# Keys' and queries' parts in an order that lets two of three come from DRAM in one transfer

## The chip, the cores and the metric

The kernel runs on one core of a Trainium2 chip. A core has a matrix engine (TensorE, PE in the profile, with its weight loads as PEld), a vector engine (DVE), a scalar engine (ACT), a general engine (POOL) and SyncE (SP), which here issues transfers. They run side by side, each in the order of its own queue, and wait for each other by semaphores. Transfers are moved by 16 DMA engines that all queues share. The metric is the time of one execution on the device in microseconds; less is better.

## What is computed

Two layers, each an attention block and a dense block with Mish, on 2048 tokens of width 512, with 32 heads of 16 columns each, in float32:

```python
def _A_ref(x, wqkv, wo):
    B, S, D = x.shape
    H = 32
    Dh = D // H
    qkv = (lambda x, *d: x.transpose(*d))((x @ wqkv).reshape(B, S, 3, H, Dh), 2, 0, 3, 1, 4)
    q, k, v = qkv[0], qkv[1], qkv[2]
    scores = jnp.einsum("bhqd,bhkd->bhqk", q, k) * (Dh ** -0.5)
    p = _softmax(scores, axis=-1)
    o = jnp.einsum("bhqk,bhkd->bhqd", p, v)
    return (lambda x, *d: x.transpose(*d))(o, 0, 2, 1, 3).reshape(B, S, D) @ wo
...
x = A_x
x = x + _A_ref(_layernorm(x, axis=-1), A_wqkv, A_wo)
x = x + _B_ref(_layernorm(x, axis=-1), B_w1, B_b1, B_w2)
x = x + _A_ref(_layernorm(x, axis=-1), A_wqkv, A_wo)
x = x + _B_ref(_layernorm(x, axis=-1), B_w1, B_b1, B_w2)
```

## The kernel before

**Numbers in two parts.** To keep float32's accuracy with the matrix engine's faster type, a number is split into a high part and a low part (the rest). A product is then the sum of three: high by high, high by low and low by high. For keys and queries the three are put below each other in the contraction: a head has 16 columns, so its keys take 48 rows and its queries 48 rows (`KROWS`), and one matmul sums all three products. `K_PARTS` and `Q_PARTS` (lines 37 and 38) say which part stands in which 16 rows: keys high, high, low and queries high, low, high. Two more rows (48 and 49, up to `MROWS` = 50) bring the row maximum into the score: ones on the keys' side, and the negated maximum, in two parts, on the queries' side.

**Projection (`qkv`, line 470).** Matmuls over the normed input make a 128x512 block of the transposed queries (m = 0 to 3) or keys (m = 4 to 7); each block holds 8 heads. `evict` (line 488) splits it into its two parts on the scalar and the vector engine and the scalar engine issues its store to `scr[m]`, a DRAM tensor of [2, 128, 2048]: part, row, token. Values go to `vscr` in the same manner.

**Loading a group (`prep_qk`, line 232).** Four heads make a group; there are 8 groups in a layer. Two heads share a tile: one in partitions 0 to 49, the other in 64 to 113. For each head SP issues a transfer of ones (line 244) and three transfers of 16 rows for the keys and three for the queries (line 251). The first group is loaded inside `qkv`, in two pieces: tokens 0 to 1535 as soon as three of the four token blocks of both `scr[0]` and `scr[4]` are stored, and the last 512 when the fourth is. Groups 1 to 7 are loaded during the group before, in `run` (line 420): `prep_qk` is a generator, and from the eighth of a group's 64 steps on, one transfer is issued in each step.

**The attention loop (`run`).** A step is one block of 512 queries by 128 keys for four heads; 16 steps make a block, four blocks a group, 512 steps a layer. Three streams are interleaved by hand in the order of `CYCLE`: row maxima (`max_pair` and `max_one`: a 128x512 score matmul at line 275, reduced by the vector engine at lines 293 and 308), scores with exponentials (line 355 on the matrix engine, 357 on the scalar engine), and products with the values (line 402). The maxima run 22 steps ahead (`AHEAD`). When a block's maxima are complete, `max_rows` (line 324) transposes them, SP writes them to DRAM (line 332, `rows<-nt`) and reads them back into rows 48 and 49 of the query tiles (line 337, `qs<-rows`); the block's scores need them.

**Order.** `Order` chains the instructions of TensorE, DVE and ACT in the order of the program. Transfers aren't chained: the compiler's scheduler places them in SP's queue by its own simulation, so that those of `prep_qk` may stand before or behind the transfers of rows.

**Layer 0 also prepares weights.** `make` (line 113) loads a block of weights, splits it, and the scalar engine issues its store; this is done at sixteen of the attention loop's steps in layer 0.

Of the kernel before, what the change touches and what calls it, by code (L numbers as in the profile page):

```python
# [10 lines left out]
F32 = mybir.dt.float32  # L11
# [9 lines left out]
S, D, H, DH, F = 2048, 512, 32, 16, 1792  # L21
NCH = 4
# [11 lines left out]
KROWS = 48  # L34
MROWS = 50
HALF = 64
K_PARTS = (0, 0, 1)
Q_PARTS = (0, 1, 0)
CYCLE = "QvXXvQMXvvXM"
TAIL_START = "QvvRvv"  # L40
TAIL = "WQRvvv"
# [10 lines left out]
def kernel(ctx: ExitStack, tc: tile.TileContext, x, wqkv, wo, w1, b1, w2, out):  # L52
    nc = tc.nc
# [20 lines left out]
    def b8(shape, dt, name):  # L74
        return blk.tile(shape, dt, tag="blk", name=name)
# [140 lines left out]
    class Attention:  # L216
# [15 lines left out]
        def prep_qk(self, g, first=0, last=S):  # L232
            l = self.l
            if g not in self.qk:
                self.qk[g] = [
                    [b8([P, S], F32R, f"{n}s{l}{g}{u}") for u in range(HG // 2)] for n in ("k", "q")
                ]
            for u in range(HG // 2):
                k, q = self.qk[g][0][u], self.qk[g][1][u]
                m, h0 = divmod(g * HG + 2 * u, P // DH)  # L240
                for e in range(2):
                    r0 = e * HALF
                    if first == 0:
                        nc.sync.dma_start(
                            k[r0 + KROWS : r0 + MROWS].bitcast(F32).rearrange("p (r n) -> p r n", n=256),
                            ones[:, None, :].to_broadcast([MROWS - KROWS, S // 256, 256]),
                        )
                        yield
                    for t, parts, base in ((k, K_PARTS, NCH), (q, Q_PARTS, 0)):
                        for j, a in enumerate(parts):  # L250
                            nc.sync.dma_start(
                                t[r0 + j * DH : r0 + (j + 1) * DH, first:last].bitcast(F32),
                                self.scr[base + m][a, (h0 + e) * DH : (h0 + e + 1) * DH, first:last].bitcast(F32),
                            )
                            yield

        def prep_v(self, g):
            va = b8([P, NKT, HG, VW], F32, f"va{self.l}{g}")
# [352 lines left out]
    def norm_steps(src, nm, got, key, tag, o):  # L611
        st = tmp.tile([P, NCH, 6], F32, tag="st", name=f"st{nm}")
        mv = tmp.tile([P, NCH, 2], F32, tag="mv", name=f"mv{nm}")
        ve = tmp.tile([P, NCH], F32, tag="ve", name=f"ve{nm}")
        rs = tmp.tile([P, NCH], F32, tag="rs", name=f"rs{nm}")
        for t in range(NCH):
            o(nc.vector.bn_stats(st[:, t], src[:, t]))
            o(nc.vector.bn_aggr(mv[:, t], st[:, t]))
            o(nc.vector.tensor_scalar(ve[:, t : t + 1], mv[:, t : t + 1, 1], EPS, None, op0=ALU.add))
            nc.gpsimd.tensor_tensor(rs[:, t : t + 1], ve[:, t : t + 1], mhalf[:, t : t + 1], op=ALU.pow)  # L620
            yield
        th = b8([P, KT, CW], F32R, f"th{nm}")
        tl = b8([P, KT, CW], F32R, f"tl{nm}")
        got[key] = (th, tl)
        xns, tps = {}, {}
        for t in range(NCH + 2):
            if t < NCH:
                xns[t] = t512("f", f"xn{nm}{t}")
                o(
                    nc.vector.tensor_scalar(  # L630
                        xns[t], src[:, t], mv[:, t, 0:1], rs[:, t : t + 1], op0=ALU.subtract, op1=ALU.mult
                    )
                )
            if t >= 2:
                hi, sp = tps.pop(t - 2)
                o(nc.vector.tensor_tensor(tl[:, :, ts(t - 2, P)], sp, hi.bitcast(F32), op=ALU.subtract))
            if 1 <= t <= NCH:
                xn, tp = xns.pop(t - 1), pbank(tag, f"tp{nm}{t - 1}")
                for k in range(KT):
                    o(nc.tensor.transpose(tp[:, ts(k, P)], xn[:, ts(k, P)], ident))  # L640
                sp = tp.rearrange("p (k n) -> p k n", k=KT)
                hi = th[:, :, ts(t - 1, P)]
                nc.scalar.activation(hi, sp, AF.Copy)
                tps[t - 1] = (hi, sp)
            yield
# [159 lines left out]
    for l in range(2):  # L805
# [18 lines left out]
        hooks, parts, work = {}, {}, {}  # L824
# [38 lines left out]
        first = norm_steps(x2s[0], f"m{l}0", tts, 0, "s", o)  # L863
# [32 lines left out]
        if l == 0:  # L896
            last = NCH - 1
# [37 lines left out]
```

## Time and profile before

| | |
|---|---|
| median of 3 runs | 3466.72 us (3463.46 to 3468.94) |
| the profiled execution, its time | 3467.81 us |
| its span | 3466.0 us |
| granted TensorE clock | 0.997 |
| HBM read, written | 149.43 MB, 92.27 MB |
| mean DMA rate over the span | 71 GB/s |

The span runs from the first to the last instruction. In a row of a group of instructions stand the line, the engine, the operation, the tiles as output<-inputs, the count, the duration and the idle time ahead of it. A name such as `ks<-scr` says that a transfer goes from `scr` to a tile of keys; SPq and ACTq are the sequencers that issue them. PEldq EVENT_SEMAPHORE is a wait of TensorE's queue ahead of a weight load, whose length tells how long it waited. The DMA share is the mean busy share of the 16 engines.

### The profile page before, as it was taken

How to read it: one execution, taken by the hardware profiler on the slowest of the kernel's cores; microseconds unless marked ns; L12 is line 12 of the kernel's file. 1: busy time of each engine (PE TensorE's matmuls, PEld its weight loads, DVE VectorE, ACT ScalarE, POOL GpSimd, SP SyncE). 2: the span in 40 equal slices, each digit the busy share in tenths (PEclk: the TensorE clock that was granted, in tenths of full speed). 3: DMA queues.
4: the chain of work that ended last, by engine and by line, in shares of the span. 5: the costliest groups of instructions: out<-in, count | busy, mean ns of one | idle time of the engine just before them, and what ended most of it. 6: DMA issues, size and time to landing. Idle time of an engine off the chain costs nothing.

```text
span 3466.0 us, 71144 instructions
## 1 busy us (share of the span) xinstructions
PE 3443.8 (99%) x29075; PEld 1917.8 (55%) x29075; DVE 2966.5 (86%) x4155; ACT 2620.2 (76%) x4865; POOL 282.1 (8%) x329
## 2 busy tenths in 40 slices
PE   9999999999999999999999999999999999999999
PEld 6644444444444445888876444444444444458887
DVE  5699999999999996665537999999999999966554
ACT  3189899989889888356522888988998999874665
POOL 1000000000000001222200000000000000012222
PEclk9999999999999999999999999999999999999999
DMA  7641312213121114500264202112020221154000
GB/s 253 233 102 35 81 43 74 61 54 81 45 58 50 37 55 109 195 13 13 86 199 156 53 15 46 26 36 43 18 56 15 46 37 25 55 136 167 13 13 25
DMA packets 131864, 247.39 MB, mean 71 GB/s; under 512 B 30929, under 2 KB 72401, under 8 KB 116433
## 3 DMA queue, kind: packets, MB, share of 16 engines
q1 hardware_dynamic: 77680, 169.43, 19.6%
q10 hardware_dynamic: 53856, 73.41, 5.8%
q8 instruction: 229, 3.75, 0.5%
q14 instruction: 99, 0.80, 0.1%
HBM read 149.43 MB, written 92.27 MB: 70 GB/s over the span
## 4 chain that ended last, share of the span: by engine, by line
PE 95%; DMA 2%; DVE 2%; ACT 1%; SPq 0%; issue 0%; DVEq 0%; ACTq 0%
PE pv L402 32%; PE sp L355 25%; PE pm L275 8%; PE pn L275 4%; PE h L165 3%; PE h L166 3%; PE h L164 3%; PE mo L164 3%; PE mo L165 3%; PE mo L166 3%; PE qk L164 1%; PE qk L165 1%; PE qk L166 1%; PE va L164 1%; PE va L166 1%; PE va L165 1%
## 5 line engine op out<-in xcount | busy, mean ns | idle before, releaser
L357 ACT ACTIVATE p<-sp 128x512 f32<-128x512 f32 x4040 | 2108.7, 599 | 240.9 <-PE pn L275 145.6
L308 DVE TENSOR_REDUCE mxv<-pn 128x1 f32<-128x512 f32 x2048 | 1306.2, 677 | 6.2 <-PE pn L275 4.4
L293 DVE TENSOR_REDUCE mxv<-pm 128x2 f32<-128x1024 f32 x1024 | 1241.8, 1213 | 78.6 <-PE pm L275 78.6
L355 PE MATMUL sp<-qs,ks 50*128 50x512 f32 x4040 | 1265.9, 445 | 0.0
L402 PE MATMUL pv<-p,va 128*32 128x256 f32 x16384 | 1211.7, 388 | 1.1 <-DVE pt L152 1.1
L355 PEld LDWEIGHTS sp<-qs,ks 50*128 50x128 f32 x4040 | 562.8, 184 | 689.2 <-ACT p L357 620.2
L275 PE MATMUL pn<-ks,qs 48*128 48x512 f32 x2048 | 824.8, 450 | 1.2 <-DVE mxv L308 0.9
L402 PEld LDWEIGHTS pv<-p,va 128*32 128x32 f32 x16384 | 385.0, 108 | 558.1 <-issue 428.4
L275 PE MATMUL pm<-ks,qs 48*128 48x512 f32 x2048 | 437.6, 423 | 1.4 <-DMA ks<-scr 1.4
L275 PEld LDWEIGHTS pn<-ks,qs 48*128 48x128 f32 x2048 | 366.2, 183 | 8.3 <-DVE mxv L308 2.7
L275 PEld LDWEIGHTS pm<-ks,qs 48*128 48x128 f32 x2048 | 193.5, 185 | 64.4 <-issue 7.8
L320 POOL CAST nh<-nm 128x16 fp32r<-128x16 f32 x64 | 12.6, 197 | 2436.7 <-DVE nm L315 2436.7
L666 POOL TENSOR_TENSOR hb<-hb,he 128x512 f32<-128x512 f32 x112 | 148.3, 1324 | 471.9 <-DVE he L663 471.9
L164 PE MATMUL mo<-w,ah 128*128 128x512 f32 x448 | 175.5, 392 | 3.2 <-ACT ah L669 3.0
L166 PE MATMUL h<-thm,w 128*128 128x512 f32 x448 | 175.0, 391 | 0.0
L165 PE MATMUL h<-tlm,w 128*128 128x512 f32 x448 | 174.9, 390 | 0.0
L165 PE MATMUL mo<-w,ah 128*128 128x512 f32 x448 | 174.9, 390 | 0.0
L164 PE MATMUL h<-thm,w 128*128 128x512 f32 x448 | 174.7, 391 | 0.0
L166 PE MATMUL mo<-w,al 128*128 128x512 f32 x448 | 166.1, 390 | 0.0
L668 DVE TENSOR_TENSOR hb<-hb,hr 128x512 f32<-128x512 f32 x112 | 77.3, 690 | 98.9 <-ACT hr L665 73.2
L151 ACT ACTIVATE pt<-qk 128x512 fp32r<-128x512 f32 x64 | 37.9, 598 | 147.7 <-PE qk L166 122.1
L660 ACT ACTIVATE hb<-h,b1t 128x512 f32<-128x512 f32 x112 | 76.9, 686 | 95.4 <-PE h L166 54.1
(133 smaller groups left out, 2590.2 us busy)
## 6 DMA issues: line engine op xcount, KB each, us to landing
scr<-pt ACTq DMA_DIRECT2D x64, 512.0 KB
ks<-scr SPq DMA_DIRECT2D x168, 128.0 KB
qs<-scr SPq DMA_DIRECT2D x168, 128.0 KB
vscr<-vst ACTq DMA_DIRECT2D x32, 512.0 KB
va<-vscr SPq DMA_DIRECT2D x16, 1024.0 KB
w<-w1p SPq DMA_DIRECT2D x14, 1024.0 KB
w<-w2p SPq DMA_DIRECT2D x14, 1024.0 KB
raw<-ot SPq DMA_DIRECT2D x256, 32.0 KB
```

The source lines that it names most:

```text
L164: pe(nc.tensor.matmul(acc, ah, bh, start=first and i == 0, stop=False))
L165: pe(nc.tensor.matmul(acc, ah, bl, start=False, stop=False))
L166: pe(nc.tensor.matmul(acc, al, bh, start=False, stop=last and i == n - 1))
L275: nc.tensor.matmul(out, qs[h // 2][rows, q0 : q0 + P], ks[h // 2][rows, ts(c, 512)], start=True, stop=True)
L293: self.order(nc.vector.tensor_reduce(self.mxs[b][:, 0:2, qt, c], pm, axis=AX.X, op=ALU.max))
L308: self.order(nc.vector.tensor_reduce(self.mxs[b][:, h, qt, c : c + 1], pm, axis=AX.X, op=ALU.max))
L355: nc.tensor.matmul(sp, ks[h // 2][rows, ts(kt, P)], qs[h // 2][rows, ts(qb, CW)], start=True, stop=True)
L357: return lambda: self.order(nc.scalar.activation(self.pts[s][:, h], sp, AF.Exp, scale=SCALE))
L402: nc.tensor.matmul(acc[ts(h, VW), cols], va[:, kt, h, :], self.pts[s][:, h, cols], start=kt == 0 and half == 0, stop=kt == NKT - 1, skip_g ...
L660: nc.scalar.activation(hb, acc, AF.Identity, bias=b1t[:, f : f + 1])
L666: nc.gpsimd.tensor_tensor(hb, hb, e, op=ALU.mult)
L668: nc.vector.tensor_tensor(hb, hb, r, op=ALU.mult)
```

## The change

In `prep_qk` the 16-row parts take another order: the keys' rows hold high, low, high, and the queries' rows high, high, low. The three products summed by the matmul are the same, and so are all tiles and matmuls. For each head and side, the high and the low part are now read from `scr` in one transfer, whose source is [2, 16, columns] and whose target is 32 neighbouring rows (rows 0 to 31 of the keys, rows 16 to 47 of the queries); a second transfer of 16 rows brings the high part again. So there are two transfers for each head and side where there were three.

```diff
-K_PARTS = (0, 0, 1)
-Q_PARTS = (0, 1, 0)
...
-                    for t, parts, base in ((k, K_PARTS, NCH), (q, Q_PARTS, 0)):
-                        for j, a in enumerate(parts):
-                            nc.sync.dma_start(
-                                t[r0 + j * DH : r0 + (j + 1) * DH, first:last].bitcast(F32),
-                                self.scr[base + m][a, (h0 + e) * DH : (h0 + e + 1) * DH, first:last].bitcast(F32),
-                            )
-                            yield
+                    for t, base, both, again in ((k, NCH, 0, 2 * DH), (q, 0, DH, 0)):
+                        src = self.scr[base + m][:, (h0 + e) * DH : (h0 + e + 1) * DH, first:last].bitcast(F32)
+                        nc.sync.dma_start(t[r0 + both : r0 + both + 2 * DH, first:last].bitcast(F32), src)
+                        yield
+                        nc.sync.dma_start(t[r0 + again : r0 + again + DH, first:last].bitcast(F32), src[0])
+                        yield
```

In the loop, each transfer is still issued in a step of its own, so a group's loads take 20 steps where they took 28.

## The prediction

> **What bounds the kernel now.** I read the page first, then the stages around each transfer that changes.
>
> ```profile
> PE 3443.8 (99%) x29075; PEld 1917.8 (55%) x29075; DVE 2966.5 (86%) x4155; ACT 2620.2 (76%) x4865; POOL 282.1 (8%) x329
> ...
> PE 95%; DMA 2%; DVE 2%; ACT 1%; SPq 0%; issue 0%; DVEq 0%; ACTq 0%
> ```
>
> TensorE is busy 99% of the span and is 95% of the chain that ended last; DMA is 2%. So removing transfers can gain little, and anything that holds TensorE up is lost in full, because its order is fixed by hand (`Order`). The span is 3466.0 us, the profiled run took 3467.8 us, 1 us over the median of 3466.72 us.
>
> The same is seen by stage. The columns are length, busy time of each engine, clock, DMA share and GB/s:
>
> ```profile
> 58.00:107.00 49.00, 47.25 (x209) 36.42 (x209) 14.99 (x21) 9.83 (x17) 0.00 (x0) 1.00 0.99 322
> 1763.00:1802.00 39.00, 38.55 (x178) 31.40 (x177) 11.00 (x17) 10.24 (x18) 0.00 (x0) 1.00 0.89 269
> ...
> 1412.00:1432.00 20.00, 20.00 (x90) 16.57 (x89) 15.19 (x29) 6.61 (x11) 4.99 (x4) 1.00 0.96 397
> ```
>
> ```profile
> 324.00:475.00 151.00, 151.00 (x1546) 68.27 (x1548) 150.86 (x202) 135.74 (x261) 11.81 (x14) 1.00 0.24 55
> ```
>
> Inside a group (324 to 475) PE and DVE are full and the DMA engines a quarter busy. While the first group's keys and queries are fetched, the DMA engines are full (0.99 in layer 0, 0.89 in layer 1). Hence one engine moves 322/(16 x 0.99) = 20.3 GB/s in that mix, and 397/(16 x 0.96) = 25.8 GB/s with long rows (1412 to 1432).
>
> **What the change removes.** The DMA view gives the transfers:
>
> ```profile
> ks<-scr SPq DMA_DIRECT2D x168, 128.0 KB
> qs<-scr SPq DMA_DIRECT2D x168, 128.0 KB
> ...
> qs<-scr SPq DMA_DIRECT2D x24, 96.0 KB
> ks<-scr SPq DMA_DIRECT2D x24, 96.0 KB
> ...
> qs<-scr SPq DMA_DIRECT2D x24, 32.0 KB
> ks<-scr SPq DMA_DIRECT2D x24, 32.0 KB
> ```
>
> That is 432 transfers; of each three, two become one of double size, so 144 go: 288 remain, half of them double. Bytes, matmuls, and evictions stay; the three products are the same with two of them swapped in the sum. The issue of one costs SP:
>
> ```profile
> L251 SPq DMA_DIRECT2D qs<-scr x216: 302/413/1872, 58.1 to 2859.0; - x108
> L251 SPq DMA_DIRECT2D ks<-scr x216: 302/418/1886, 62.4 to 2855.4; - x108
> ...
> who waited for it (us, times):
>   ACT pt L151: 7.6, 3
> ...
>   PE pm L275: 1.4, 1
> ```
>
> 144 x 0.415 = 60 us of SP's time, but SP sits waiting: 1207 us for the maxima's transpose alone.
>
> ```profile
> SPq L332 <- DVE nt L329: 1207.1, 64, 24.7
> ```
>
> The only wait of TensorE on these transfers is 1.4 us, once. So what is removed is worth 0 to 1.4 us.
>
> **What it adds.** Now each transfer's outermost extent is its 16 rows, on both sides. The merged one reads DRAM as [2, 16, columns]: outermost extent 2, into 32 rows. If the work is dealt out along the outermost extent, only 2 of the 16 DMA engines get any. No row here shows a long transfer of that shape, so I bound it. Over 16 engines a merged 256 KB transfer is 16,384 B an engine, 0.6 us at 25.8 GB/s. Over two it is 131,072 B, 5.1 us (6.5 at 20.3). I take two: the only shape that differs from all long transfers of the trace is the one that would have to be cut along its 16 rows instead of along its first extent, on one side alone. [...]
>
> *First group, layer 0.* SP issues, and the matmuls that need the data:
>
> ```profile
> 58.15 2.31 SPq L251 DMA_DIRECT2D qs<-scr  x5
> 62.40 2.64 SPq L251 DMA_DIRECT2D ks<-scr  x6
> ...
> 95.93 2.44 SPq L251 DMA_DIRECT2D qs<-scr  x3
> ```
>
> ```profile
> 67.80 0.47 PE L275 MATMUL pm<-ks,qs 48*128 48x512 f32 x1 [1.42 <-DMA ks<-scr]
> ```
>
> ```profile
> 84.92 0.49 PE L275 MATMUL pn<-ks,qs 48*128 48x512 f32 x2
> ```
>
> ```profile
> 106.81 0.50 PE L275 MATMUL pm<-ks,qs 48*128 48x512 f32 x2
> ```
>
> The first maximum at 67.80 already waits for its data. The one at 84.92 needs heads 2 and 3, the one at 106.81 the last 512 columns. Eight merged transfers of 192 KB put 98,304 B on each of the two engines, 4.8 us at 20.3 GB/s; eight of 64 KB put 32,768 B, 1.6 us: together 51 us, and the sixteen single ones 3 us more. From 58.15 they are through at 112, 5 us behind the need at 106.81, if nothing else ran there. The rest of that window, (322 GB/s x 49 us - 3.1 MB)/16 = 0.79 MB an engine, is 39 us more, which would make it 44 us late. I take the middle, **25 us**; part of it comes early, at 67.80, where three merged transfers stand ahead instead of a few short ones. What waits behind the stalled maximum is all of TensorE's queue, and DVE's reduction with it.
>
> *First group, layer 1.* The transfers start at 1762.85, the maxima later:
>
> ```profile
> 1762.85 3.13 SPq L251 DMA_DIRECT2D qs<-scr  x6
> ...
> 1800.06 1.55 SPq L251 DMA_DIRECT2D qs<-scr  x3
> ```
>
> ```profile
> L275 PE MATMUL pm<-ks,qs x12: 493/493/493, 1819.5 to 1837.6; 48*128 48x512 f32 x12
> ```
>
> Six pairs 3.6 us apart: the fourth, which needs the last columns, is at 1830.4. The same 54 us give 1817, in time; with the other (269 x 39 us - 3.1 MB)/16 = 0.46 MB, 23 us, 1840, 10 us late. In both layers the scalar engine issues the stores of `scr` and was held up by these loads already (7.6 us, three times, above): loads that land later hold evictions, and so TensorE, longer. Bounds 0 and 25; I take **10 us**.
>
> *Groups 1 to 7, both layers (14 times).* The burst for group 2:
>
> ```profile
> 359.20 1.70 SPq L332 DMA_DIRECT2D rows<-nt  x4
> 361.01 0.82 SPq L251 DMA_DIRECT2D qs<-scr  x2
> 362.06 1.12 SPq L337 DMA_DIRECT2D qs<-rows  x4
> 363.22 2.00 SPq L251 DMA_DIRECT2D qs<-scr  x4
> ...
> 373.94 0.68 SPq L244 DMA_DIRECT2D ks<-ones  x1
> 374.66 1.32 SPq L251 DMA_DIRECT2D ks<-scr  x3
> 376.03 0.64 SPq L244 DMA_DIRECT2D ks<-ones  x1
> 376.72 1.39 SPq L251 DMA_DIRECT2D ks<-scr  x3
> 378.21 4.09 SPq L251 DMA_DIRECT2D qs<-scr  x6
> ```
>
> ```profile
> L355 PEldq EVENT_SEMAPHORE  x4: 51/51/51, 366.2 to 367.1; - x4
> ```
>
> ```profile
> 396.78 1.69 SPq L332 DMA_DIRECT2D rows<-nt  x4
> 399.55 1.11 SPq L337 DMA_DIRECT2D qs<-rows  x4
> ```
>
> The maxima's rows (`qs<-rows`) of the next block go out at 362.06 behind two query transfers and are asked for by four score matmuls at 366.2 to 367.1, which did not wait. A small transfer takes about 1.1 us to land (rows issued by 398.47, read back from 399.55). With a merged one and a single one ahead, the engines are free at 361.01 + 1.1 + 5.1 + 0.3 = 367.5, and the rows are there near 368: 1.6 us late, 3.0 at the slower rate. If both heads' merged transfers go ahead, 7 us; if none, 0. I take 2 us, **28 us** in all (0 to 98). The burst at 374 holds four merged ones, 20 us: through by about 397, just ahead of the rows of 396.78, so I cost it at nothing; its cover is those 2 us, and beyond them each us counts. The next group's maxima begin 42 of 64 steps into the group, 16 steps being 37.6 us (359.20 to 396.78) and the group's first scores 37.6 us before 366.2: near 427, clear. Layer 0's sixteen weight stores are issued by the scalar engine; if a quarter meet a burst and wait 1.2 us, **5 us** (0 to 30).
>
> Sum: -0 + 25 + 10 + 28 + 5 = 68 us on 3467.8, or 3536; 3535 against the median.
>
> **Rivals.**
> - *The merged transfer spreads over all 16 engines, so it isn't slower.* Then everything above is nil; the removed issues are off the path and at most the 1.4 us wait goes, with as much again at later waits: 3464 to 3469. For it: same bytes and two clean blocks of 16 rows. Against: the extent of 2. It decides where the first maximum (67.80) stands: if it starts no later, this is the case. Chance 0.17, of which 0.13 within 0.2% and 0.04 faster; that the merged copy is cut in two again when it is compiled gives the same time and is in it.
> - *Two engines, but hidden.* The share of 0.24 in a group speaks for it; the full DMA engines and the 1.4 us wait at the first group against. Only 0 to 7 us, 3468 to 3474: 0.04.
> - *Two engines, and the upper ends*: rows behind two merged transfers in every group, evictions waiting for loads, 44 + 25 + 98 + 30 = 197 us, 3665; half way, from 3600 on, 0.10. For it: the rows have 1 us to spare in the burst above.
> - The forecast, 3475 to 3600: 0.69.
>
> **How the numbers follow.** A measurement of this kernel tells 0.2%, 7 us, from no change. Slower by more: 0.69 + 0.10 = 0.79. Within: 0.13 + 0.04 = 0.17. Faster: 0.04. The forecast's own range is 3475 to 3600; to leave out no more than 2 in 10 the range takes in the first rival's upper part, 3464 to 3600.
>
> **What would show it.** Right: the first maximum of layer 0 starts at 73 or later with a wait on `ks<-scr` or `qs<-scr`, and the maximum now at 106.81 at 120 or later; while bursts run the mean DMA share is near 2/16; score matmuls wait on `qs<-rows` once in most groups, some 2 us; blocks otherwise stay 37.6 us apart. Wrong: the first maximum near 67, or the rows sent ahead of the queries. My sum is most exposed where the schedule puts the rows in SP's queue, and in how two queues share a busy DMA engine.

## The result, and the profile after

The changed kernel takes 3557.2 us (median) where the kernel before takes 3465.1 us: a ratio of 1.026, with a 95% interval of 1.0249 to 1.0274. It is 92 us slower. Slower was forecast, with 68 us; 3557 lies in the range of 3464 to 3600.

The page of the changed kernel. Its lines are 2 or 3 lower than before: 249 issues the merged transfers, 251 the single ones, 329 and 334 the maxima's rows, 352 the score matmuls, 272 those of the maxima.

```profile
PE 3472.4 (98%) x29075; PEld 1931.5 (54%) x29075; DVE 2969.0 (83%) x4155; ACT 2621.0 (74%) x4865; POOL 282.0 (8%) x329
...
q1 hardware_dynamic: 73360, 169.41, 15.0%
...
PE 81%; DVE 10%; DMA 7%; SPq 1%; ACT 1%; issue 0%; DVEq 0%; ACTq 0%
```

The work is the same. In the chain that ended last, DMA has gone from 2% to 7% and TensorE from 95% to 81%. The packets of SP's queue (q1) tell what the merged transfers do. There are 4320 fewer of them (77,680 before), 30 for each of the 144 transfers removed, and they are small ones: the page counts 30,929 packets under 512 B before and 26,608 after. The counts fit a transfer that shows its 32 or 16 rows as packets and, besides, one small packet for each engine that it ran on: two of 16 rows on 16 engines make 32 + 32, so a merged one makes 34, 32 rows and two small ones. Over 16 engines it would be 48, and 2304 packets fewer in all.

Where the time went can be read by comparing the same event in both kernels. First the score matmuls of before and of after, with the first and the last start of each line (352 and 376 are 355 and 379 before; the second of each runs only at the end of a layer):

```profile
L355 PEld LDWEIGHTS sp<-qs,ks x4040: 182/183/332, 172.2 to 3098.5; 50*128 50x128 f32 x193
...
L379 PEld LDWEIGHTS sp<-qs,ks x56: 182/183/183, 1332.0 to 3098.1; 50*128 50x128 f32 x56
```

```profile
L352 PEld LDWEIGHTS sp<-qs,ks x4040: 182/183/330, 207.0 to 3190.2; 50*128 50x128 f32 x193
...
L376 PEld LDWEIGHTS sp<-qs,ks x56: 182/183/183, 1396.9 to 3189.8; 50*128 50x128 f32 x56
```

Then the writes of a block's rows, once in each layer. Before they were at 396.78 (above) and, in layer 1:

```profile
1935.14 1.69 SPq L332 DMA_DIRECT2D rows<-nt  x4
```

After, in layer 0 and in layer 1:

```profile
433.79 1.69 SPq L329 DMA_DIRECT2D rows<-nt  x4
```

```profile
2025.45 1.70 SPq L329 DMA_DIRECT2D rows<-nt  x4
```

| event | before | after | late by | lost in the stage |
|---|---|---|---|---|
| layer 0's first scores | 172.2 | 207.0 | 34.8 | |
| rows of layer 0's block 6 | 396.78 | 433.79 | 37.0 | layer 0's start: 37 |
| layer 0's last scores, first of them | 1332.0 | 1396.9 | 64.9 | layer 0's later groups: 28 |
| rows of layer 1's block 1 | 1935.14 | 2025.45 | 90.3 | layer 1's start: 25 |
| layer 1's last scores | 3098.1 | 3189.8 | 91.7 | layer 1's later groups: 1.4 |

This compares one execution with one, so a stage's size is good to a few microseconds. The first row of sizes holds more than the start, too: the loads of group 1 stand ahead of block 6, and after them the rows of block 1 land late and its scores wait.

```profile
241.12 1.70 SPq L329 DMA_DIRECT2D rows<-nt  x4
248.46 1.13 SPq L334 DMA_DIRECT2D qs<-rows  x4
```

With merged transfers in the first groups alone (a run below), block 6's rows are written 29.9 us late instead of 37:

```profile
426.69 1.69 SPq L335 DMA_DIRECT2D rows<-nt  x4
```

So about 30 of the 37 us are the start's own, and some 7 come with the merged loads of group 1.

**Layer 0's start.** Two tables of what waited for what, before (56 to 107) and after (56 to 140), in the stretch of the first group's loads; columns are engine and line, releaser, total, times, longest:

```profile
ACT pt L151 <- DMA qs<-scr: 4.9, 2, 3.0
```

```profile
ACT pt L149 <- DMA qs<-scr: 25.7, 3, 9.0
...
PE pm L272 <- DMA ks<-scr: 10.8, 2, 6.3
PE pn L272 <- DMA qs<-scr: 10.6, 1, 10.6
```

The maxima wait 21 us for keys and queries. More than that, the scalar engine waits 26 us for loads of queries at line 149, which does not read queries: it evicts a projection. Ahead of each eviction it issues the store of an earlier one to `scr`:

```profile
60.98 0.62 SPq L249 DMA_DIRECT2D qs<-scr  x1
...
73.79 0.37 ACTq L488 DMA_DIRECT2D scr<-pt  x1
74.26 0.60 ACT L149 ACTIVATE pt<-qk 128x512 fp32r<-128x512 f32 x1 [8.97 <-DMA qs<-scr]
```

Why a store waits for a load that it has nothing to do with stands in the trace. Each transfer signals its landing by one of eight semaphores (101 and 103 to 109 in this stretch), SP's and the scalar engine's transfers use them in turn, and none of the transfers from 56 to 140 is issued before the one that used its semaphore last has landed. The store at 73.79 has number 109, last used by the merged load of queries issued at 60.98. The next two, at 83.93 and 93.57, follow merged loads issued at 68.27 and 75.05 in the same way; the evictions behind them waited 9.55 us for `ks<-scr` and 9.04 us for `qs<-scr`. So in this stretch loads that land late hold evictions, and TensorE behind them. The windows (length, busy time of each engine, clock, DMA share, GB/s) show the two starts, and a later group's burst, as a whole:

```profile
59.00:140.00 81.00, 53.20 (x203) 40.27 (x202) 14.59 (x21) 9.83 (x17) 0.00 (x0) 0.81 0.56 199
1828.00:1895.00 67.00, 48.03 (x196) 37.59 (x194) 10.91 (x17) 9.84 (x17) 0.00 (x0) 0.87 0.46 161
561.00:591.00 30.00, 30.00 (x312) 13.54 (x308) 29.96 (x42) 26.72 (x52) 0.42 (x2) 1.00 0.33 108
```

TensorE does in 81 us about what it did in 49 (203 matmuls against 209). The DMA share is 0.56 where it was 0.99, though the loads are what everything waits for; that fits a few full engines beside idle ones.

**Layer 1's start** is the same by the other road. The maxima's keys and queries are there in time, and their matmuls wait for no transfer:

```profile
L272 PE MATMUL pm<-ks,qs x16: 493/493/493, 1913.6 to 1938.9; 48*128 48x512 f32 x16
```

But the evictions ahead of them are late (waits from 1835 to 1895), again behind stores that wait for loads:

```profile
DVE pt L150 <- ACT pt L149: 41.2, 8, 10.0
...
PE qk L162 <- ACT thq L640: 12.5, 1, 12.5
ACT pt L149 <- DMA qs<-scr: 10.2, 1, 10.2
```

**Layer 0's later groups.** The loads of group 3, and the rows behind them:

```profile
561.89 0.59 SPq L249 DMA_DIRECT2D ks<-scr  x1
...
563.68 0.59 SPq L249 DMA_DIRECT2D ks<-scr  x1
...
564.91 0.61 SPq L249 DMA_DIRECT2D qs<-scr  x1
...
566.03 0.60 SPq L249 DMA_DIRECT2D qs<-scr  x1
571.11 0.31 SPq L251 DMA_DIRECT2D qs<-scr  x1
572.11 0.40 SPq L115 DMA_DIRECT2D w1r<-in_B_w_dram  x1
584.10 2.51 SPq L329 DMA_DIRECT2D rows<-nt  x4
593.45 1.11 SPq L334 DMA_DIRECT2D qs<-rows  x4
```

```profile
595.01 0.78 PE L352 MATMUL sp<-qs,ks 50*128 50x512 f32 x2 [3.43 <-DMA qs<-rows]
```

Four merged loads, and a block of weights behind them. The writes of the rows were issued by 586.6 and had landed only at 593.45, 6.8 us later instead of 1.1. The scores stood still for 3.4 us. While the rows were waited for, the DMA engines were almost idle on average:

```profile
588.00:593.00 5.00, 3.58 (x38) 1.47 (x36) 5.00 (x7) 3.46 (x7) 0.00 (x0) 1.00 0.12 45
```

A share of 0.12 is as much as two full engines of 16. Their 45 GB/s, 22.5 each, lie between the 20.3 and 25.8 that the prediction worked out for a busy engine, and far under the 397 GB/s from 1412 to 1432 in the kernel before. So neither DRAM nor the sixteen engines together were full. This happens in eight blocks, in pairs (blocks 10 and 11, 13 and 14, 22 and 23, 25 and 26 of layer 0), 2 to 4.5 us each, and the wait at block 1 above is of the same kind.

### The profile page after: what moved, and what is told of

The parts are those of the page before. It is cut to its first block, busy times and chain, and to the rows that moved or that the text cites. A ratio compares the mean times of both kernels' runs of the same rounds, so it can differ in the third digit from the quotient of the medians.

```text
span 3557.4 us, 71007 instructions
## 1 busy us (share of the span) xinstructions
PE 3472.4 (98%) x29075; PEld 1931.5 (54%) x29075; DVE 2969.0 (83%) x4155; ACT 2621.0 (74%) x4865; POOL 282.0 (8%) x329
## 2 busy tenths in 40 slices
DMA packets 127542, 247.37 MB, mean 70 GB/s; under 512 B 26608, under 2 KB 68080, under 8 KB 112112
## 3 DMA queue, kind: packets, MB, share of 16 engines
q1 hardware_dynamic: 73360, 169.41, 15.0%
## 4 chain that ended last, share of the span: by engine, by line
PE 81%; DVE 10%; DMA 7%; SPq 1%; ACT 1%; issue 0%; DVEq 0%; ACTq 0%
PE pv L399 26%; PE sp L352 21%; PE pm L272 6%; DVE mxv L305 4%; DVE mxv L290 4%; PE pn L272 4%; PE h L163 3%; PE h L164 3%; PE h L162 3%; DMA qs<-scr 3%; PE mo L162 3%; PE mo L163 3%; PE mo L164 3%; PE qk L162 1%; DMA rows<-nt 1%; DMA scr<-pt 1%
## 5 line engine op out<-in xcount | busy, mean ns | idle before, releaser
L272 PE MATMUL pn<-ks,qs 48*128 48x512 f32 x2048 | 828.3, 452 | 11.8 <-DMA qs<-scr 10.6
```

What stands on the lines that cost most here:

```text
L272: nc.tensor.matmul(out, qs[h // 2][rows, q0 : q0 + P], ks[h // 2][rows, ts(c, 512)], start=True, stop=True)
```

## The experiments

Theory: a merged transfer, whose source has the two parts as its outermost extent, is moved by 2 of the 16 DMA engines, and that alone is the loss. Rivals: the part order or the new order in SP's queue; the size of the transfers, whatever their shape; in the later groups the merged loads alone, without the weights.

**The parts' order alone.**

```diff
-for t, base, both, again in ((k, NCH, 0, 2 * DH), (q, 0, DH, 0)):
...
+for t, base, parts in ((k, NCH, (0, 1, 0)), (q, 0, (0, 0, 1))):
+    for j, a in enumerate(parts):
+        nc.sync.dma_start(t[r0 + j * DH : r0 + (j + 1) * DH, first:last]..., self.scr[base + m][a, ...])
```

> Parts in the new order (keys high, low, high; queries high, high, low), but three transfers of 16 rows as before: the merging alone is undone. Theory (a merged transfer runs on two of 16 DMA engines): 3462 to 3470 us, q1 back at about 77700 packets, each block of scores where it stood before. Rival (the part order, and with it another order in SP's queue, costs the time): near 3557 us.

Measured: 3464.6 us, ratio 0.9998 (0.9989 to 1.0007). q1 is back at 77,680 packets. The order costs nothing; the merging does.

**As few transfers, with 16 outermost.**

```diff
+src = self.scr[base + m][:, (h0 + e) * DH : (h0 + e + 1) * DH, first:last].bitcast(F32)
+if base:
+    pairs, rest = src.rearrange("a r n -> r a n"), src[0]
+else:
+    pairs, rest = src[0].unsqueeze(1).to_broadcast([DH, 2, last - first]), src[1]
+nc.sync.dma_start(t[r0 : r0 + 2 * DH, first:last].bitcast(F32), pairs)
+nc.sync.dma_start(t[r0 + 2 * DH : r0 + 3 * DH, first:last].bitcast(F32), rest)
```

> As few transfers as the changed kernel, two for each head and side, but the 32-row one has its 16 rows as outermost extent: keys' high and low part of a row stand next to each other (source [16, 2, columns]), queries read the high part twice by a source with a repeated extent ([16, 2 x the same row, columns]). Theory (outermost extent 2 confines the transfer to two engines): 3460 to 3470 us, q1 packets 144 x 16 under the kernel before, about 75400. Rival (a transfer of 256 KB, or the fewer issues and their other places in the queue, hold up the rest whatever its shape): 3520 to 3560 us.

Measured: 3464.4 us, ratio 1.0003 (0.9994 to 1.0013), and in the queue's row:

```profile
q1 hardware_dynamic: 75376, 169.42, 18.2%
```

That is 2304 packets fewer than before, 144 x 16, the count above for 16 engines. They are as large and as many as in the changed kernel, and the loss of 92 us is gone. Size and number are out as causes. Nor is anything gained: 144 transfers fewer are worth nothing that can be measured.

**The first group alone, and the later groups alone.** The merged transfer is kept where a condition holds; elsewhere its two parts are read by two transfers.

```diff
+if g == 0:          # the second run: g > 0
+    nc.sync.dma_start(t[r0 + both : r0 + both + 2 * DH, first:last].bitcast(F32), src)
+else:
+    for a in range(2):
+        nc.sync.dma_start(t[row : row + DH, first:last].bitcast(F32), src[a])
```

> New part order in all groups; the merged transfers only in the first group of each layer, three transfers in groups 1 to 7. Theory (losses are local to the stage and add up): the layers' starts keep their 37 and 25 us, the later groups lose nothing: 3465 + 62 = 3527 us (3515 to 3537). Rival (later groups wait because the start left them behind, or the start waits only for what the later groups queue): over 3545 or under 3500 us.

> New part order in all groups; the merged transfers only in groups 1 to 7 of each layer. Theory: the layers' starts are as before, layer 0's later groups lose 28 us and layer 1's 1 to 2: 3465 + 29 = 3494 us (3484 to 3504). Rival (a stall in a group is absorbed by the next): 3465 to 3475 us.

Measured: 3522.7 us (ratio 1.0172, 1.0155 to 1.0189) and 3496.7 us (1.0095, 1.0080 to 1.0110). They are 59 and 33 us over the kernel before; 92 together, as the change. The stages add up, and a stall in one isn't absorbed by the next.

**The weights moved**, on the changed kernel and on the one before.

```diff
-hooks[30 + 24 * n] = lambda kind=kind, i=i: make(kind, i)
+hooks[GSTEPS * (n // 3) + (38, 46, 54)[n % 3]] = lambda kind=kind, i=i: make(kind, i)
```

> The changed kernel, with layer 0's sixteen weight blocks prepared at steps 38, 46 and 54 of groups 0 to 5 instead of every 24th step. In the changed kernel layer 0 lost 28 us in four pairs of blocks (10 and 11, 13 and 14, 22 and 23, 25 and 26), which are those of groups where a weight block falls on step 22 or 6, beside the merged loads. Theory (merged loads leave the two engines just enough room, and a weight load or store in the same stretch pushes the rows' transfers over their time): the pairs vanish, layer 0's later groups lose under 5 us, total 3525 to 3537 us. Rival (the merged loads alone delay the rows in those groups): 3550 to 3560 us, the pairs where they were.

> The kernel before with the same move of the weight blocks, as the control. Both theories: 3460 to 3470 us; if the move itself costs or gains, it shows here and is taken off the run on the changed kernel.

Measured: 3533.2 us on the changed kernel, 24 us less than it had; 3463.6 us on the kernel before, ratio 0.9996 (0.9987 to 1.0006). The rows of the block that stood still in the changed kernel:

```profile
571.15 0.31 SPq L251 DMA_DIRECT2D qs<-scr  x1
584.36 1.70 SPq L329 DMA_DIRECT2D rows<-nt  x4
588.92 1.11 SPq L334 DMA_DIRECT2D qs<-rows  x4
```

They are back 2.9 us after the write instead of 6.8, and all four pairs are gone. So in a later group the merged loads alone nearly fit. With a block of weights beside them they don't. The wait at block 1 stays, where weights are still loaded just ahead of group 1's merged loads in this run too.

**The rows by another queue.**

```diff
-nc.sync.dma_start(rows[:, :, :, j, :]..., nt[32 * j : 32 * j + 32, :])
+nc.gpsimd.dma_start(rows[:, :, :, j, :]..., nt[32 * j : 32 * j + 32, :])
...
-nc.sync.dma_start(qs[h // 2][r : r + 2, ts(qb, CW)]..., rows[:, h]...)
+nc.gpsimd.dma_start(qs[h // 2][r : r + 2, ts(qb, CW)]..., rows[:, h]...)
```

> The changed kernel, with the maxima's rows written and read back through GpSimd's queue instead of SP's. Theory (the rows wait in SP's order behind merged loads on two engines): the four pairs of stalls in layer 0 vanish; what GpSimd's slower issue costs is the same in every block and shows in all 64 blocks alike; 3525 to 3540 us if that is hidden. Rival (the stalls come from the scalar engine or from a full DRAM, not from the queue's order): the pairs stay, 3550 us or more.

Measured: 3651.5 us, ratio 1.0535 (1.0515 to 1.0556). The theory's range of 3525 to 3540 is missed by far. As the rival had it, the four pairs stay, and many other blocks now lose time as well. In a block without loads beside it, and in one with them (GpSimd's queue):

```profile
364.90 2.04 POOL L329 DMA_DIRECT2D rows<-nt  x4 [4.50 <-DVE nt L326]
368.66 2.07 POOL L334 DMA_DIRECT2D qs<-rows  x4 [1.72 <-DMA rows<-nt]
```

```profile
600.04 2.04 POOL L329 DMA_DIRECT2D rows<-nt  x4 [4.50 <-DVE nt L326]
607.23 1.99 POOL L334 DMA_DIRECT2D qs<-rows  x4 [5.15 <-DMA rows<-nt]
```

GpSimd takes 2 us for four issues, where SP took 1.7 and 1.1, and its wait for the rows is 1.7 us in the one and 5.2 in the other. A queue of their own does not take the rows past the merged loads, so the order within SP's queue is not what holds them. The rival's two causes, the scalar engine or a full DRAM, are not shown either: the DMA engines moved only 55 GB/s, at a share of 0.15, from 602 to 607.3, while these rows were waited for. What is left is that the rows' transfers also need the two engines that are full, which the run fits but doesn't show by itself. How much of the 94 us over the changed kernel is GpSimd's own cost was not taken apart.

**The first piece alone.** As the first group alone, with the condition `g == 0 and first == 0`.

> New part order; merged transfers only in the first piece (tokens 0 to 1535) of the first group of each layer, three transfers everywhere else. The run with the whole first group merged lost 59 us. Theory (time goes with the bytes that the two engines have to move): the first piece has three quarters of them, so 44 us, 3500 to 3516 us. Rival by the prediction's own step (most is lost where the last 512 columns are needed): under 3490 us.

Measured: 3510.4 us, ratio 1.0133 (1.0114 to 1.0152), 47 us over before and four fifths of the 59 us for the whole group. That is near the first piece's share of the bytes, three quarters, and it isn't what the prediction's own sum had, in which most is lost at the last 512 columns.

**Extents 8 and 4, and a control.** From the kernel with 16 outermost, in the first group only:

```diff
+rows = 8 if g == 0 else DH          # the second run: 4
+for i in range(0, DH, rows):
+    nc.sync.dma_start(t[r0 + 2 * i : r0 + 2 * (i + rows), first:last].bitcast(F32), pairs[i : i + rows])
...
+w = (last - first) // (4 if g == 0 else 1)          # the control
+for i in range(0, last - first, w):
+    nc.sync.dma_start(t[r0 : r0 + 2 * DH, first + i : first + i + w].bitcast(F32), pairs[:, :, i : i + w])
```

> The kernel with 16 as outermost extent; in the first group of each layer each of its 32-row transfers is cut into two with outermost extent 8. Theory (the engines used are as many as the outermost extent, and the start's loss goes with the bytes that the busiest engine moves over an even share, 1/8 - 1/16 against 1/2 - 1/16 for extent 2, which lost 59 us): at most 59 x 0.0625/0.4375 = 8 us, less what slack there is: 3463 to 3473 us. Rival (extents under 16 all cost alike): near 3523 us.

> The same, cut into four with outermost extent 4 in the first group. Theory: at most 59 x 0.1875/0.4375 = 25 us, less slack of the order of 5 to 10 us a layer: 3468 to 3490 us, between extent 8 and extent 2. Rival (the number of transfers is what costs): as the run with four column pieces.

> The control for the last: in the first group each 32-row transfer is cut into four by columns, so there are as many transfers, each with outermost extent 16. Theory: 3462 to 3472 us, since every engine has its even share. Rival (the number of transfers costs): 3470 to 3490 us, with extent 4.

Measured, each against the kernel before in the same runs (3466.7 us):

| outermost extent in the first group | us | ratio (interval) |
|---|---|---|
| 8, two transfers | 3466.5 | 0.9999 (0.9990 to 1.0009) |
| 4, four transfers | 3498.7 | 1.0089 (1.0074 to 1.0104) |
| 16, four transfers of a quarter of the columns | 3477.9 | 1.0037 (1.0024 to 1.0049) |

Extent 8 costs nothing and extent 4 costs 32 us. The queue's packets fit the number of engines: 75,376 in both runs, since two transfers on 8 engines or four on 4 make 16 small packets as one on 16 does. Extent 4 lies above the theory's range of 3468 to 3490. The control, in which by the theory every engine has its even share, was expected at 3472 us at most, and its 3477.9 falls to the rival: pieces cost something even with 16 outermost. But the control cuts more than the number: its rows are four times shorter, and q1 has 79,984 packets. So its 11 us can't be put down to the number of transfers alone. With all of them taken off extent 4's 32 us, 21 are left for the extent, where 59 x 0.1875/0.4375 = 25 was the bound. That a smaller outermost extent costs more holds for these three: 0 us for 8, 21 to 32 for 4, 59 for 2.

## Why the prediction was right, point by point

- **What bounds the kernel** was right: what is taken away from DMA gains nothing (the kernel with 16 outermost), and what holds TensorE is lost in full (59 + 33 = 92).
- **Removed: 0 to 1.4 us.** Right; 3464.4 us with the same transfers removed.
- **A merged transfer runs on two engines.** No row of before showed the count; two was the author's choice, and no run shows the engines of a transfer one by one. The runs fit two: 30 packets fewer for a merged transfer with 2 outermost and 16 fewer with 16, a DMA share of 0.12 (two engines would make 0.125) while the rows were waited for, and 3464.4 us for the kernel with 16 outermost against 3557.2 us. The first rival falls with that, and so does the second, in which the transfers are hidden.
- **Layer 0's start, 25 us: mis-sized; measured 37 with group 1's loads, about 30 without them.** "I take the middle" was the weak step. The signs came: the first maximum was to start at 73 or later, and started at 79.1; the one at 106.81 at 120 or later, and started at 141.6.

```profile
79.09 0.76 PE L272 MATMUL pm<-ks,qs 48*128 48x512 f32 x1 [6.29 <-DMA ks<-scr]
...
141.59 0.50 PE L272 MATMUL pm<-ks,qs 48*128 48x512 f32 x2
```

  But the path was another. The sum was worked out from the last 512 columns, and their maximum, at 141.59, waited for no transfer. The 35 us were lost before it: in waits for the first piece (the maximum of heads 2 and 3 came at 103.81 instead of 84.92) and in evictions, held by the scalar engine's stores (26 us of waits for loads of queries, 5 before). The prediction names the evictions for both layers, under layer 1, but put no price on them in layer 0's sum.
- **Layer 1's start, 10 us: mis-sized; measured 25**, the upper bound. The prediction worked it out from the need of the last columns, which did not wait, and named the evictions only beside it. They were the path. That a store waits for a load stands in the trace, by the shared semaphores; what it costs in us was not taken apart by a run.
- **Later groups, 28 us: the sum came near (29.4 by the table, 33 by the run with the later groups alone), the mechanism half.** The prediction had the rows read back (`qs<-rows`) behind one query load in every group, 14 times 2 us. The schedule put all query loads ahead of the rows' write. So it is the write that lands late, and SP's wait for it grew from 70.5 to 149.0 us:

```profile
SPq L337 <- DMA rows<-nt: 70.5, 69, 3.1
```

```profile
SPq L334 <- DMA rows<-nt: 149.0, 82, 6.7
```

  Most blocks have room for that. The burst of four merged loads, which was costed "at nothing" with 2 us of cover, is the one that costs, where a weight block takes the cover away: 28 us in eight blocks of layer 0, next to nothing in layer 1, which prepares no weights. That the total agrees is luck: 14 groups of 2 us were forecast.
- **Weight stores held up, 5 us:** the weights matter, but not so. Their sixteen waits in the scalar engine's queue lasted 17 ns each, and with the weights moved 24 us came back through the rows.

```profile
L128 ACTq EVENT_SEMAPHORE  x16: 17/17/17, 293.5 to 1159.3; - x16
```

- **DMA share near 2/16 in a burst:** wrong for a burst as a whole, 0.33 at 561 and 0.56 at layer 0's start, where other traffic is mixed in; right in the stretch in which the rows were waited for, 0.12.

So the step that failed is the price of the layers' starts, 25 + 10 = 35 us, worked out from the last columns instead of the first piece and the evictions; the run with merged transfers there alone lost 59. The later groups with their weights were forecast at 28 + 5 = 33 us, and the run with those alone lost 33.

## What to carry to other kernels

What a merged transfer was worth here hung on its outermost extent: 3557.2 us with the two parts outermost, 3464.4 us with the 16 rows. At the 45 GB/s of the stretch above, 256 KB would take some 6 us, an estimate, and the rows written behind four such loads and a block of weights landed after 6.8 us instead of 1.1. If parts are to be joined, put the long extent first (here the rows, with the two parts inside), and compare the packet count of the queue: 73,360 with 2 outermost, 75,376 with 16. And where the engine that bounds the kernel is 99% busy, ask of fewer transfers not what the issues cost, but whether any of them was waited for.

## What the runs showed of the hardware that was not expected

TensorE's granted clock fell where the loads made it wait: 0.81 over layer 0's start (0.55 from 75 to 90, 0.73 from 90 to 105) and 0.87 over layer 1's, against 1.00 in both before. After the wait for queries that ended at 103.81 matmuls start 0.42 us apart (105.22 and 105.64):

```profile
103.81 0.89 PE L272 MATMUL pn<-ks,qs 48*128 48x512 f32 x2 [10.64 <-DMA qs<-scr]
104.63 0.79 PE L162 MATMUL qk<-thq,qkm 128*128 128x512 f32 x1
105.22 0.63 PE L163 MATMUL qk<-tlq,qkm 128*128 128x512 f32 x1
105.64 0.63 PE L164 MATMUL qk<-thq,qkm 128*128 128x512 f32 x1
```

In a stretch without waits they start 0.23 us apart (140.82, 141.04 and 141.27):

```profile
140.82 0.39 PE L162 MATMUL va<-vm,thq 128*128 128x512 f32 x1
141.04 0.39 PE L163 MATMUL va<-vm,thq 128*128 128x512 f32 x1
141.27 0.39 PE L164 MATMUL va<-vm,tlq 128*128 128x512 f32 x1
```

So here the 10.6 us of that wait were not all: the matmuls behind it started at little over half the pace of the later stretch. What this cost in us was not taken apart by a run. The other surprise is the control's 11 us: cutting loads with 16 rows outermost into four pieces of shorter rows took 3477.9 us against 3466.7.
